# RWKV attention and routed experts in one kernel: a unit's scores masked in blocks of 64 tokens, the bonus term put on their diagonal

## The chip, the cores and the metric

The kernel runs as one program on one core of a Trainium2 chip. The metric is the device time of one execution in microseconds (us), taken as the median of several runs; lower is better. Engines are called PE (TensorE), DVE (VectorE), ACT (ScalarE), POOL (GpSimd) and SP (SyncE, which here only issues DMAs and reads registers). PSUM is the memory that PE writes into, in banks of 512 float32 columns on 128 partitions; SBUF holds everything else.

## What is computed

An RWKV attention over 4 batches, 8 heads of 48, 768 tokens, and then a mixture of 8 experts in which each of the 3072 tokens goes to one expert:

```python
for t in range(S):                                   # attention, per batch and head
    kt, vt, rt = k[:, :, t], v[:, :, t], r[:, :, t]
    cur = einsum('bhd,bhe->bhde', u * kt, vt)
    y[:, :, t] = einsum('bhd,bhde->bhe', rt, state + cur)
    state = w[..., None] * state + einsum('bhd,bhe->bhde', kt, vt)
x = y as (3072, 384)
logits = x @ w_gate + modality_bias[modality_id]     # experts
e_idx = argmax(logits); gate_w = softmax(logits)[e_idx]
for e in range(8):
    mask = e_idx == e
    out[mask] = gate_w[mask] * (relu(x[mask] @ w1[e]) @ w2[e])
```

## The kernel before, in words

The attention is computed in 24 units of 128 tokens (one of 4 batches, one of 6 chunks). Token t's own key enters with the factor u, all earlier ones of the chunk with powers of w; chunks before it come in through a state of 48 x 48 per head. A unit's value is so a sum of three parts: scores of the chunk with itself, masked to s < t, times v; the state times r; and the diagonal part, d v, where d is a number per token and head (the sum of r u k, "bonus").

For unit i the parts are, with the names that the code and the trace use:

- `keys_turned` and `keys` (L349, L399): k turned by PE into `pkT`, multiplied on DVE by powers of w into `kc`. `rc` (L361, POOL) is r with such powers.
- `scores` (L442): 16 matmuls of 64 keys by 128 tokens into two banks `psc` (heads of even number in one, of odd number in the other; the two partition halves of `kc` that hold them are two row halves of PE).
- `causal` (L448): two DVE products of 128x512 with the mask, out of PSUM into `at`.
- `values`: into the bank `py` first the state part (L472, eight matmuls, 96 columns), then `at` times v (L479, 16 matmuls of 128 keys, 64 tokens, 48 columns); then into the bank `pst` the state of the next chunk (L488 the old one faded, L493 keys times values; for units 4 to 13 both are on PE), and in the same bank the bonus of the next unit (L408).
- `taken` (L416): DVE copies the bonus out of `pst` as `d`. `own` (L428): ACT multiplies v by d, head by head, into `dv` (eight products of 128x48); for units 9 to 13 POOL does the second half (L424).
- `token` (L501, L516): DVE adds `dv` to `py`, then ACT squares the row and sums it. A power of two near its size (`factor`, L311 and L313 on DVE, `sx`) scales the row, which is kept as two float16 halves: `high` on ACT (L549), `low` on DVE (L553). `raised` (L562) turns it on PE, `flipped` (L577) copies it out on ACT.
- `settled_state` (L531, L539): ACT copies the new state from `pst` to `st`.

The order on each engine is written by hand in `run`: it is a loop over units, and in iteration i unit i's values stand beside unit i+1's scores and masks, unit i−1's row, unit i+2's keys, unit i+3's `rc`. All instructions of an engine run in the order in which they are written. Two or three "fills" in an iteration take the next instruction of a generator that computes routing (logits, the expert of a token, its place, its send to DRAM with an indirect DMA on POOL). In iterations 9 to 13 the weights of the first expert are split too, each sixth of them by ACT into `whi` (L1000) and by DVE into `wlo` (L1005); loads of these weights are issued by SP in iterations 3 to 10 (`halves`), after SP has waited for `d` and `sx` of the unit (`pace`). From 165 us on only experts' work is left.

In the setup and the first iterations run the small tables: `wd` (L217, four ACT products) and `tri` (L220), the faded state's factors and a triangle used in routing; their generator is drained by the same fills, behind `first`, which computes where the experts' rows begin.

Of the kernel before, what the change touches and what calls it, by code (L numbers as in the profile page):

```python
# [9 lines left out]
F32 = mybir.dt.float32  # L10
# [8 lines left out]
P = 128  # L19
# [6 lines left out]
E = 8  # L26
# [20 lines left out]
SHARED = range(9, 14)  # L47
TURNED = range(1, 15)
RAISED = range(4, 12)
OWNED = range(17, 24)  # L50

# [14 lines left out]
class _Kernel:  # L66
# [16 lines left out]
    def setup(self):  # L83
# [58 lines left out]
        nc.gpsimd.affine_select(self.mask, self.ones, pattern=[[1, P]], compare_op=ALU.is_gt, fill=0.0, base=0, channel_multiplier=-1)  # L142
        self.counts()
# [266 lines left out]
    def taken(self, i):  # L410
        u = self.ctx_[i]
        u["d"] = self.a.tile([P, H], F32, tag="d", name=f"d{i}", bufs=4)
        if i in OWNED:
            self.nc.vector.reduce_sum(u["d"], u["rk"].rearrange("p (h e) -> p h e", e=D), axis=AX.X)
            return
        self.nc.vector.tensor_copy(u["d"], u["pd"])  # L416

    def own(self, i, q):
        nc, u = self.nc, self.ctx_[i]
        if q == 0:  # L420
            u["dv"] = self.a.tile([P, DM], F32, tag="dv", name=f"dv{i}")
        if q and i in SHARED:
            half = lambda t: t[:, DM // 2 :].rearrange("p (h e) -> p h e", e=D)
            nc.gpsimd.tensor_mul(half(u["dv"]), half(u["v"]), u["d"][:, H // 2 :].unsqueeze(2).to_broadcast([P, H // 2, D]))  # L424
            return
        for h in range(q * H // 2, (q + 1) * H // 2):
            sl = slice(h * D, (h + 1) * D)
            nc.scalar.activation(u["dv"][:, sl], u["v"][:, sl], AF.Copy, scale=u["d"][:, h : h + 1])  # L428

    def scores(self, i):  # L430
# [7 lines left out]
        for pr in range(NPR):  # L438
            for q in range(2):
                s = slice(64 * q, 64 * q + 64)  # L440
                for j, r in enumerate(HALVES):
                    nc.tensor.matmul(u["ps"][j][s, pr * P : (pr + 1) * P], u["kc"][r, pr, s], u["rc"][r, pr, :], start=True, stop=True)  # L442

    def causal(self, i, j):
        nc, u = self.nc, self.ctx_[i]
        if j == 0:
            u["at"] = self.a.tile([P, H, P], F32, tag="at", name=f"at{i}")
# [14 lines left out]
    def values(self, i, beside=lambda: None):  # L462
# [3 lines left out]
        py = u["py"] = self.ps_y.tile([P, 512], F32, tag="y", name=f"py{i}")  # L466
        if c:
            for pr in range(NPR):
                c0 = pr * 2 * D
                for q in range(2):  # L470
                    t = slice(64 * q, 64 * q + 64)
                    nc.tensor.matmul(py[t, c0 : c0 + 2 * D], u["rc"][:112, pr, t], st[:112, b, pr, :], start=pr == 0, stop=False, skip_group_check=True)  # L472

        for h in range(H):
# [22 lines left out]
    def token(self, i):  # L497
# [3 lines left out]
        nc.vector.tensor_add(u["x"], u["x"], u["dv"])  # L501
# [87 lines left out]
    def choose(self, u):  # L589
# [7 lines left out]
        xinv = a.tile([P, B, 2], F32, tag="xinv", name=f"xinv{lo}")[:, :n, 0]  # L597
# [3 lines left out]
        nc.vector.reduce_sum(L, lg.rearrange("p g w e -> p g e w"), axis=AX.X)  # L601
        yield
        nc.vector.scalar_tensor_tensor(L, L, self.wginv, eb(xinv), ALU.mult, ALU.mult)
# [6 lines left out]
        bank = lambda c, w=E: u["pr"][:, c : c + n * w].rearrange("p (g w) -> p g w", g=n)  # L610
# [14 lines left out]
        zs = new("zs", 1)  # L625
# [19 lines left out]
    def place(self, u):  # L645
# [9 lines left out]
        pos = a.tile([P, B], F32, tag="pos", name=f"pos{lo}")[:, :n]  # L655
# [501 lines left out]
    def run(self):  # L1157
# [26 lines left out]
        def plan(step, f):  # L1184
            at.setdefault(step, []).append(f)
# [6 lines left out]
        halves = {3: (0, 1), 4: (2,), 5: (3, 4), 6: (5,), 7: (6,), 8: (7, 8), 9: (9, 10), 10: (11,)}  # L1192

        def half(i, at):
            for q in halves.get(i, ())[at : at + 1]:
                if q == 0:
                    self.eid = nc.sync.value_load(self.ctl[:, :1], min_val=0, max_val=E - 1)
                self.load(self.eid, 2 * NQ, q)
# [8 lines left out]

        routing = self.setup2()
        plan(0, lambda: next(routing))
        plan(1, lambda: next(routing))  # L1210
        plan(1, lambda: fills.append(chain(self.first(), routing, self.first_order())))
# [355 lines left out]
```

## Time and profile before

| | us |
|---|---|
| three runs | 340.17, 343.05, 343.06 |
| median | 343.05 |
| the profiled execution's own time | 344.49 |
| its span | 342.8 |
| PE busy | 325.1 (95% of the span) |
| DVE busy | 216.1 (63%) |
| ACT busy | 180.6 (53%) |
| POOL busy | 161.8 (47%) |

The span runs from the first to the last instruction that the profile holds; some 1.7 us of the execution lie outside it. The units take about the first 165 us, the experts the rest. Busy PE means that a matmul is in flight, at either of the two clock levels; the granted clock says how far it ran below 2.4 GHz.

### The profile page before, as it was taken

To read this page: it belongs to the slowest core of one execution; us is meant where nothing else is said; L and a number is where in the kernel's file an instruction comes from. 1 tells how busy PE (TensorE), PEld (TensorE's weight loads), DVE (VectorE), ACT (ScalarE), POOL (GpSimd) and SP (SyncE) were. 2 spreads that over 40 slices of the span, in tenths; PEclk is the share of its full clock that TensorE was granted. 3 is DMA by queue.
4 is the path that set the end of the run, shared out by engine and by line. 5 is a ranking of instruction groups with operands and counts; after the bars stand their busy time and mean duration, and the time that the engine had idled before them with its cause. 6 is when DMAs were issued, how large, how long until landed. Compare 5 with 4: busy or idle time off the path is not lost. (4 is left out here: it accounts for less than half of the span.)

```text
span 342.8 us, 15268 instructions
## 1 busy us (share of the span) xinstructions
PE 325.1 (95%) x5471; PEld 264.7 (77%) x5471; DVE 216.1 (63%) x748; ACT 180.6 (53%) x483; POOL 161.8 (47%) x237
## 2 busy tenths in 40 slices
PE   8997999889999999999998999998999999999992
PEld 3787888788888888797886788876888877777671
DVE  8966986989997987787666523377333332333950
ACT  7759799685874758577421222264222225542820
POOL 8967787986949786344458211202211111111211
PEclk9999999989999999999999999999999999999998
DMA  6767967655799999973366541118512211122110
GB/s 187 233 144 207 248 228 225 207 156 132 169 219 205 270 283 235 217 175 96 86 110 240 148 72 46 46 46 288 154 46 63 52 46 23 46 68 47 36 46 5
DMA packets 56414, 47.55 MB, mean 139 GB/s; under 512 B 40744, under 2 KB 49207, under 8 KB 56112
## 3 DMA queue, kind: packets, MB, share of 16 engines
q1 hardware_dynamic: 53168, 37.45, 45.7%
q0 software_dynamic: 3200, 9.47, 7.6%
q8 instruction: 31, 0.51, 0.6%
q14 instruction: 15, 0.12, 0.1%
HBM read 27.21 MB, written 11.83 MB: 114 GB/s over the span
## 5 line engine op out<-in xcount | busy, mean ns | idle before, releaser
L1059 PEld LDWEIGHTS <-whi 128*128 128x128 f16 x1248 | 72.4, 98 | 4.3 <-issue 1.0
L1068 DVE SCALAR_TENSOR_TENSOR hl<-phb,hh 128x256 f16<-128x256 f32 (+1 forms) x48 | 24.5, 511 | 69.6 <-issue 36.4
L1122 PEld LDWEIGHTS <-hh 128*128 128x128 f16 x416 | 39.0, 98 | 28.6 <-ACT hh L1063 2.0
L1059 PE MATMUL phb<-mxT,whi 128*128 128x128 f16 x768 | 51.0, 219 | 0.2
L428 ACT ACTIVATE dv<-kv,d 128x48 f32<-128x48 f32 x172 | 43.1, 325 | 1.1 <-DVE d L416 1.0
L1063 ACT ACTIVATE hh<-phb 128x256 f16<-128x256 f32 (+1 forms) x48 | 21.4, 454 | 41.0 <-PE phb L1059 18.6
L1059 PEld LDWEIGHTS <-wlo 128*128 128x128 f16 x624 | 37.8, 98 | 0.0
L1028 POOL TENSOR_TENSOR seenb<-otb,putb 128x1 int32<-128x1 int32 x16 | 4.4, 273 | 66.7 <-ACTq L1498 53.2
L448 DVE TENSOR_TENSOR at<-psc,mask 128x512 f32<-128x512 f32 x48 | 31.8, 681 | 0.2 <-PE psc L442 0.2
L685 POOL DMA_INDIRECT rows<-row,posi x24 | 26.5, 1105 | 11.0 <-DVE base L661 3.1
L1122 PEld LDWEIGHTS <-hl 128*128 128x128 f16 x208 | 19.4, 98 | 15.3 <-issue 2.5
L361 POOL TENSOR_TENSOR rc<-ud,powr 112x512 f32<-112x512 f32 (+1 forms) x25 | 30.6, 1226 | 0.8 <-PE py L472 0.4
L1122 PE MATMUL po<-whi,hh 128*128 128x384 f16 x136 | 27.7, 326 | 2.0 <-ACT whi L1000 1.2
L1059 PE MATMUL phb<-mxT,wlo 128*128 128x128 f16 x384 | 29.3, 219 | 0.0
L1122 PE MATMUL po<-whi,hl 128*128 128x384 f16 x136 | 28.0, 326 | 1.2 <-PEq L1563 0.7
L442 PE MATMUL psc<-rc,kc 48*64 48x128 f32 (+1 forms) x768 | 27.8, 280 | 0.2
L1122 PE MATMUL po<-wlo,hh 128*128 128x384 f16 x136 | 27.7, 326 | 0.0
L1059 PE MATMUL phs<-mxT,whi 128*128 128x128 f16 x432 | 27.2, 219 | 0.0
L1019 ACT ACTIVATE otb<-po,fac 128x384 f32<-128x384 f32 x16 | 9.3, 579 | 33.8 <-PE phb L1059 33.8
L479 PE MATMUL py<-kv,at 128*64 128x48 f32 x768 | 26.9, 223 | 0.0
L1005 DVE SCALAR_TENSOR_TENSOR wlo<-raw,ws,whi 128x1024 f16<-128x1024 f32 (+1 forms) x20 | 25.9, 1313 | 1.3 <-issue 0.6
L442 PEld LDWEIGHTS psc<-rc,kc 48*64 48x64 f32 (+1 forms) x768 | 21.3, 134 | 6.2 <-issue 2.8
(288 smaller groups left out, 639.2 us busy)
## 6 DMA issues: line engine op xcount, KB each, us to landing
kv<-in_pt SPq DMA_DIRECT2D x21, 384.0 KB
ud<-in_pd SPq DMA_DIRECT2D x10, 384.0 KB
raw<-in_w SPq DMA_DIRECT2D x12, 256.0 KB
raw<-in_w SPq DMA_DIRECT2D x6, 512.0 KB
raw<-in_w SPq DMA_DIRECT2D x2, 1536.0 KB, 6.4
ud<-in_pd SPq DMA_DIRECT2D x14, 192.0 KB
rows<-pad SPq DMA_DIRECT2D x10, 193.0 KB
rt<-in_pt SPq DMA_DIRECT2D x7, 192.0 KB
```

Source lines behind the costliest of these rows:

```text
L361: nc.gpsimd.tensor_mul(u["rc"][:TOP, s], u["rT"][:TOP, s], self.powr[:TOP, s])
L428: nc.scalar.activation(u["dv"][:, sl], u["v"][:, sl], AF.Copy, scale=u["d"][:, h : h + 1])
L442: nc.tensor.matmul(u["ps"][j][s, pr * P : (pr + 1) * P], u["kc"][r, pr, s], u["rc"][r, pr, :], start=True, stop=True)
L448: nc.vector.tensor_mul(u["at"][:, j * NPR : (j + 1) * NPR, :], u["ps"][j].rearrange("p (q t) -> p q t", q=NPR), self.mask.unsqueeze(1).to_ ...
L479: nc.tensor.matmul(py[t, sl], u["at"][:, j * NPR + pr, t], u["v"][:, sl], start=c == h == 0, stop=h == H - 1, skip_group_check=True)
L685: i = nc.gpsimd.indirect_dma_start(out=self.rows, out_offset=bass.IndirectOffsetOnAxis(ap=u["posi"][:, b : b + 1], axis=0), in_=u["row"][: ...
L1005: self.nc.vector.scalar_tensor_tensor(self.wlo[:, sl], self.raw[:, sl], sc, self.whi[:, sl], ALU.mult, ALU.subtract)
L1019: self.nc.scalar.activation(ot, po[:, :DM], AF.Copy, scale=gf[:, t : t + 1])
L1059: self.nc.tensor.matmul(ph[:, q * P : (q + 1) * P], w[:, c0 : c0 + P], self.xT[:, xq, t * P : (t + 1) * P], start=i == q == 0, stop=i == l ...
L1063: self.nc.scalar.activation(self.hh[:, f0 : f0 + fb, t * P : (t + 1) * P], p3, AF.Relu)
L1068: self.nc.vector.scalar_tensor_tensor(self.hl[:, f0 : f0 + fb, r], p3, 0.0, self.hh[:, f0 : f0 + fb, r], ALU.max, ALU.subtract)
L1122: self.nc.tensor.matmul(po[:, :DM], h[:, f, t * P : (t + 1) * P], w[:, c0 : c0 + DM], start=first, stop=last)
```

## The change

`BANDED` is the set of units 9 to 13; for them

- the masked scores are no longer one 128 x 128 block per head. They are kept as `band`, the two 64 x 64 blocks on the diagonal (the keys of the same 64 tokens, one above the other on the partitions), and `past`, the block of the later 64 tokens with the earlier 64 keys, which needs no mask. The block above the diagonal isn't computed.
- `scores` writes 64 instead of 128 columns for the second half of the keys, and its result is laid out by block, head and token.
- `causal` multiplies on DVE only `band` (128x256 for each bank) with a 64-column mask; ACT copies `past` (64x256 for each bank). The lower half of `past` is zeroed by POOL, for units 9 and 10 only: `at` becomes two fixed tiles used in turn.
- `taken` puts the bonus on the diagonal of `band` by a predicated copy on DVE (mask `eye`, 128x512) out of the bank `pst`, instead of copying 128x8.
- `own` does nothing (no `dv`), and `token` has no add.
- `values` begins with 16 matmuls of `band` (64 keys, 64 tokens, 48 columns), then the state part, then eight of `past` (128 partitions, 64 tokens, 48 columns).

For all units: `eye` and the 64-column mask are four ACT copies in the setup; small results of routing (`xinv`, `zs`, `pos`) lie in PSUM columns and the sum of the logits in SBUF; the generator with `wd` and `tri` is interleaved with steps 2 to 6 of `first`; and the loads of the first expert's weight halves begin one slot later.

```diff
-SHARED = range(9, 14)
+BANDED = range(9, 14)
@@ setup
+        self.att = [c.tile([P, H, P], F32, name=f"at{q}") for q in range(2)]
+        self.band, self.eye = (c.tile([P, P // 2], F32, name=n) for n in ("band", "eye"))
+        for q in range(2):
+            t = slice(64 * q, 64 * q + 64)
+            nc.scalar.copy(self.eye[t], id32[t, t])
+            nc.scalar.copy(self.band[t], self.mask[t, t])
@@ taken
+        if i in BANDED:
+            to = [P, 2, NPR, P // 2]
+            self.nc.vector.copy_predicated(
+                u["band"].rearrange("p (j a) t -> p j a t", j=2),
+                self.eye.bitcast(I32).unsqueeze(1).unsqueeze(1).to_broadcast(to),
+                u["pd"].rearrange("p (a j) -> p j a", j=2).unsqueeze(3).to_broadcast(to),
+            )
+            return
@@ own
+        if i in BANDED:
+            return
-        if q and i in SHARED:
-            half = lambda t: t[:, DM // 2 :].rearrange("p (h e) -> p h e", e=D)
-            nc.gpsimd.tensor_mul(half(u["dv"]), half(u["v"]), u["d"][:, H // 2 :].unsqueeze(2).to_broadcast([P, H // 2, D]))
-            return
@@ scores
+                    if i in BANDED:
+                        to = u["ps"][j][s].rearrange("p (w a t) -> p w a t", w=2, a=NPR)[:, : 2 - q, pr]
+                        nc.tensor.matmul(to, u["kc"][r, pr, s], u["rc"][r, pr, 64 * q :].rearrange("p (w t) -> p w t", w=2 - q), start=True, stop=True)
+                        continue
@@ causal
-            u["at"] = self.a.tile([P, H, P], F32, tag="at", name=f"at{i}")
+            u["at"] = self.att[i % 2]
+        if i in BANDED:
+            if j == 0 and i - 2 not in BANDED:
+                nc.gpsimd.memset(u["past"][64:], 0.0)
+            s, half = slice(j * NPR, (j + 1) * NPR), u["ps"][j].rearrange("p (w a t) -> p w a t", w=2, a=NPR)
+            nc.vector.tensor_mul(u["band"][:, s], half[:, 0], self.band.unsqueeze(1).to_broadcast([P, NPR, P // 2]))
+            nc.scalar.copy(u["past"][:64, s], half[:64, 1])
+            return
@@ values
+        for h in range(H if i in BANDED else 0):
+            pr, j = divmod(h, 2)
+            sl = slice(h * D, (h + 1) * D)
+            for t in (slice(0, 64), slice(64, P)):
+                nc.tensor.matmul(py[t, sl], u["band"][t, j * NPR + pr, :], u["v"][t, sl], start=h == 0, stop=False, skip_group_check=True)
...
+            nc.tensor.matmul(py[64:, sl], u["past"][:, j * NPR + pr, :], u["v"][:, sl], start=False, stop=h == H - 1, skip_group_check=True)
@@ token
-        nc.vector.tensor_add(u["x"], u["x"], u["dv"])
+        if i not in BANDED:
+            nc.vector.tensor_add(u["x"], u["x"], u["dv"])
@@ choose
-        xinv = a.tile([P, B, 2], F32, tag="xinv", name=f"xinv{lo}")[:, :n, 0]
+        xinv = col(448)
-        nc.vector.reduce_sum(L, lg.rearrange("p g w e -> p g e w"), axis=AX.X)
+        raw = new("lgs")
+        nc.vector.reduce_sum(raw, lg.rearrange("p g w e -> p g e w"), axis=AX.X)
@@ run
-        halves = {3: (0, 1), 4: (2,), 5: (3, 4), 6: (5,), 7: (6,), 8: (7, 8), 9: (9, 10), 10: (11,)}
+        halves = {3: (None, 0), 4: (1, 2), 5: (3, 4), 6: (5,), 7: (6,), 8: (7, 8), 9: (9, 10), 10: (11,)}
-        plan(1, lambda: fills.append(chain(self.first(), routing, self.first_order())))
+        plan(1, lambda: fills.append(chain(beside(self.first(), routing, 2, 5), routing, self.first_order())))
```

On DVE, in iteration 10, the rows around the split of a sixth of the first expert's weights (`wlo`). Before:

```order
L1005 SCALAR_TENSOR_TENSOR wlo<-raw,ws,whi 128x1024
L501 TENSOR_TENSOR py_1509<-py_1509,dv_1492 128x384
L827 TENSOR_SCALAR skip<-again_1507 128x1
L416 COPY d_1622<-pst_1534 128x8
L598 TENSOR_SCALAR xinv_1632<-sx_877 128x4
```

After, as far as the masked products of the next unit:

```order
L1041 SCALAR_TENSOR_TENSOR wlo<-raw,ws,whi 128x1024
L863 TENSOR_SCALAR skip<-again_1501 128x1
L424 COPY_PREDICATED at_157<-eye,pst_1536 128x512
L634 TENSOR_SCALAR pr_1561<-sx_887 128x4
L855 TENSOR_SCALAR done<-done,fur_0_1482 128x1
L405 TENSOR_TENSOR kc_1639<-pkT_1596,powk 112x512
L317 TENSOR_SCALAR ebx_1641<-ssq_1444 128x1
L638 TENSOR_REDUCE lgs_1643<-pr_1561 128x32
L319 TENSOR_SCALAR sx_1445<-ebx_1641 128x1
L857 TENSOR_SCALAR off<-done 128x1
L469 TENSOR_TENSOR at_158<-psc_0_1601,band 128x256
L640 SCALAR_TENSOR_TENSOR pr_1561<-lgs_1643,wginv,pr_1561 128x32
```

The add behind `wlo` is gone, the predicated copy stands where the small copy of `d` stood, and the masked product has 256 columns instead of 512.

On PE, the values of unit 10, between the scores of unit 11 (`psc`) and the faded state (`pst` from `wd`). Before:

```order
L442 MATMUL psc_0_1599<-rc_1326,kc_1474 64x128
L442 MATMUL psc_1_1600<-rc_1326,kc_1474 64x128
L472 MATMUL py_1668<-st_98,rc_1189 64x96 x8
L479 MATMUL py_1668<-kv_89,at_1498 64x48 x16
L488 MATMUL pst_1693<-st_98,wd 64x48
```

After:

```order
L456 MATMUL psc_0_1601<-rc_1323,kc_1472 64x64
L456 MATMUL psc_1_1602<-rc_1323,kc_1472 64x64
L495 MATMUL py_1663<-kv_89,at_157 64x48 x16
L501 MATMUL py_1663<-st_98,rc_1188 64x96 x8
L506 MATMUL py_1663<-kv_89,at_157 64x48 x8
L521 MATMUL pst_1696<-st_98,wd 64x48
```

The 16 matmuls with `at` stand ahead of the state part instead of behind it (they are those of `band`), and eight more, those of `past`, stand behind it.

On ACT, the end of iteration 2 and the beginning of iteration 3. Before:

```order
L531 COPY st_99<-pst_461 48x4x48
L428 ACTIVATE dv_543<-kv_91,d_518 128x48 x4
L549 ACTIVATE row_402<-py_444,sx_405 128x384
L428 ACTIVATE dv_543<-kv_91,d_518 128x48 x4
L516 ACTIVATE row_402,ssq_404<-py_562 128x384
L531 COPY st_99<-pst_579 64x4x48
L217 ACTIVATE wd<-id_150,w_186 112x112
L531 COPY st_99<-pst_579 48x4x48
L217 ACTIVATE wd<-id_150,w_186 112x112 x3
```

After:

```order
L565 COPY st_99<-pst_466 48x4x48
L223 ACTIVATE wd<-id_150,w_194 112x112 x3
L440 ACTIVATE dv_552<-kv_91,d_523 128x48 x4
L583 ACTIVATE row_408<-py_449,sx_411 128x384
L223 ACTIVATE wd<-id_150,w_194 112x112
L226 CAST tri<-mask 128x128
L440 ACTIVATE dv_552<-kv_91,d_523 128x48 x4
L550 ACTIVATE row_408,ssq_410<-py_573 128x384
L565 COPY st_99<-pst_590 64x4x48
```

All of `wd` and `tri` stand one iteration earlier: in front of and between the products of `dv`, no longer between the state copies.

## Rows read from the trace of the kernel before

**Rows 1.** The page's busy times of each engine, with share and instructions.
```profile
PE 325.1 (95%) x5471; PEld 264.7 (77%) x5471; DVE 216.1 (63%) x748; ACT 180.6 (53%) x483; POOL 161.8 (47%) x237
```

**Rows 2.** Windows by stage; columns as in its second line.
```profile
core 0: us, PE busy (x) PEld busy (x) DVE busy (x) ACT busy (x) POOL busy (x), PEclk, DMA share, GB/s
...
59.00:75.00 16.00, 13.61 (x343) 12.37 (x340) 15.08 (x47) 11.99 (x32) 14.39 (x14) 0.89 0.59 184
75.00:98.00 23.00, 22.54 (x550) 20.09 (x546) 22.36 (x66) 15.92 (x39) 16.62 (x15) 1.00 0.74 166
98.00:165.00 67.00, 66.96 (x1306) 56.14 (x1306) 53.01 (x185) 44.16 (x142) 41.26 (x51) 1.00 0.90 209
```

**Rows 3.** Windows: five units, and two pieces of unit 10 and 11's iterations.
```profile
56.85:91.54 34.69, 31.85 (x810) 29.38 (x809) 31.70 (x99) 26.24 (x66) 28.94 (x27) 0.95 0.61 174
66.13:70.39 4.26, 2.61 (x59) 2.18 (x59) 4.26 (x16) 4.23 (x9) 3.82 (x5) 1.00 0.92 272
70.39:74.64 4.25, 4.25 (x81) 3.92 (x82) 3.33 (x14) 3.12 (x11) 3.94 (x5) 0.60 0.33 99
```

**Rows 4.** Timeline of PE, 56 to 83: unit 9's values, then waits of iteration 10.
```profile
57.99 0.88 PE L472 MATMUL py<-st,rc 112*64 112x96 f32 x16
58.70 1.09 PE L479 MATMUL py<-kv,at 128*64 128x48 f32 x32
59.62 0.57 PE L488 MATMUL pst<-st,wd 112*64 112x48 f32 x15
...
66.13 0.61 PE L488 MATMUL pst<-st,wd 112*64 112x48 f32 x15 [0.74 <-ACT st L539]
...
69.68 0.34 PE L562 MATMUL pxT<-id,row 128*128 128x128 f16 x3 [1.01 <-DVE row L553]
```

**Rows 5.** Waits, 56 to 98: us in total, times, longest.
```profile
ACT row L516 <- DVE py L501: 9.8, 5, 3.5
```

**Rows 6.** Timeline of DVE, 59 to 75.
```profile
60.46 0.67 DVE L448 TENSOR_TENSOR at<-psc,mask 128x512 f32<-128x512 f32 x1
...
62.07 2.40 DVE L1005 SCALAR_TENSOR_TENSOR wlo<-raw,ws,whi 128x1024 f16<-128x1024 f32 x1
64.39 0.55 DVE L501 TENSOR_TENSOR py<-py,dv 128x384 f32<-128x384 f32 x1
...
64.92 0.15 DVE L416 COPY d<-pst 128x8 f32<-128x8 f32 x1
64.99 1.43 DVE L598 TENSOR_SCALAR xinv<-sx 128x4 int32<-128x4 int32 x1
...
69.71 1.26 DVE L1005 SCALAR_TENSOR_TENSOR wlo<-raw,ws,whi 128x1024 f16<-128x1024 f32 x1
```

**Rows 7.** Timelines: DVE late in the kernel, and POOL from 59 to 70.
```profile
168.30 0.16 DVE L598 TENSOR_SCALAR xinv<-sx 128x3 int32<-128x3 int32 x1
...
200.63 0.42 DVE L1068 SCALAR_TENSOR_TENSOR hl<-pha,hh 128x256 f16<-128x256 f32 x1
...
62.09 1.28 POOL L361 TENSOR_TENSOR rc<-ud,powr 112x512 f32<-112x512 f32 x1
...
65.38 1.00 POOL L368 TENSOR_TENSOR kt<-kv,wtok 128x384 f32<-128x384 f32 x1
```

**Rows 8.** Timeline of ACT, 56 to 72: iteration 10.
```profile
65.46 0.62 ACT L539 COPY st<-pst 64x192 f32<-64x192 f32 x2
66.10 0.80 ACT L577 COPY xT<-pxT 128x768 f16<-128x768 f16 x1
...
67.71 0.56 ACT L549 ACTIVATE row<-py,sx 128x384 f16<-128x384 f32 x1
68.18 1.14 ACT L1000 ACTIVATE whi<-raw,ws 128x1024 f16<-128x1024 f32 x1
```

**Rows 9.** Timeline of PE, 17.9 to 20.8: single matmuls with 128 columns of weights.
```profile
17.96 0.38 PE L213 MATMUL pswg<-wgssq,ones 128*128 128x1 f32 x2
18.20 0.63 PE L349 MATMUL pkT<-id,kv 128*112 128x128 f32 x4
```

**Rows 10.** Timeline of PE, 26 to 46: start, busy, line, idle before.
```profile
29.97 0.88 PE L472 MATMUL py<-st,rc 112*64 112x96 f32 x16 [0.41 <-DVE wgs L313]
...
32.35 0.61 PE L488 MATMUL pst<-st,wd 112*64 112x48 f32 x15 [0.58 <-ACT st L531]
...
37.55 0.61 PE L488 MATMUL pst<-st,wd 112*64 112x48 f32 x15 [0.20 <-ACT st L539]
...
45.50 0.34 PE L562 MATMUL pxT<-id,row 128*128 128x128 f16 x3 [0.26 <-DVE row L553]
```

## What the change is predicted to do

> **What bounds the kernel now.** I read the page's busy times first, then the windows by stage, then the PE timeline, the waits, and the other engines where PE stood. PE is busy 95% of the span, the next engine, DVE, 63% [rows 1]. So a unit is worth what PE does in it, plus what PE waits. The stages differ: from 75 to 98 us PE leaves 0.46 of 23 us open, from 98 to 165 us 0.04 of 67, but from 59 to 75 us 2.39 of 16, and there DVE is busy 15.08 of 16 and the granted clock averages 0.89 [rows 2]. Since PE has next to no slack from 83 us on, what is won or lost before carries to the end.
>
> PE multiplies with `at` of units 9 to 13 in the stretch 56.85 to 91.54 us: 34.69 us, PE busy 31.85, so 2.84 idle. In 70.39 to 74.64 the granted clock was 0.60, that is, for much of it the lower level of 1.2 GHz, right after a stretch in which PE was busy for 2.61 of 4.26 us [rows 3]. The work in that slow piece (scores, state, at·v) took 4.25 us; in iteration 9 it took 59.62 − 56.85 = 2.77 [rows 3, 4], of which some 0.1 was a matmul of the expert weights' scale: 1.59 lost. There are four waits of over 0.3 us in this stretch (those at 66.13 and 69.68 stand in the rows), and each also hides some 0.2 us in which the last matmul's drain counts as busy. Sum: 2.84 + 1.59 + 4 × 0.2 = **5.2 us** that PE loses there; its bare work is 29.5 us, or 5.9 a unit.
>
> What is late there? PE at 66.13 waits for ACT's state copy, at 69.68 for DVE's half of `row` [rows 4], and between them for ACT's half. ACT's own large wait is the Square behind DVE's add of `dv`: five times, 9.8 us, the longest 3.5 [rows 5]. And that add is late because `wlo` is ahead of it on DVE: 2.40 us beside POOL's `rc` at 62.09, with the add at 64.39 [rows 6, 7]. So the chain is wlo, add, Square, state copy, PE.
>
> **Removed.** In each of five units: DVE's add, 0.55 [rows 6]; four ACT products for one half of `dv` and POOL's one product for the other. None is PE work, so alone they are worth only PE's waits behind them. With the add gone Square and the state copies behind it no longer stand behind `wlo` through the add. But the predicated copy now stands in the same place on DVE, behind `wlo`, and reads the bank that the state copy reads. I take it that ACT waits for it, where today it waits for the 0.15 copy of `d` only after the add [rows 6].
>
> **Added on DVE.** The two masked products shrink from 128x512 to 128x256: 0.67 [rows 6] against 0.42, the nearest 256-column row [rows 7]; 2 × 0.25 = 0.5 off. The copy of `d`, 0.15, becomes a predicated copy of 128x512. No row has one: bounds 0.42 (as 256 columns) and 1.35 (twice a 512-column row); I take 0.70, nearest to the 512-column product that also reads PSUM and a broadcast. DVE per unit: −0.55 − 0.5 + (0.70 − 0.15) = −0.5. Since DVE has no slack at 59 to 75 us, that is 0.5 more air where PE waits.
>
> **Added on ACT.** Two past copies of 64x256, about 0.35 each by the 64x192 state copies, 0.31 [rows 8], against four products less: no heavier. In the iteration before unit 9 ACT gets only the copies, +0.7, hidden by Square's waits, of which the mean is 9.8 / 5 = 2 us [rows 5]. Two memsets on POOL follow `kt` of the next unit, three units ahead of the need; unhidden they would cost the first past matmul of units 9 and 10 at most a `kt` each, 1.0 [rows 7]. Four copies in the setup sit beside DVE's decay tables; uncovered, 0.3 each by the same state copies.
>
> **PE.** Old at·v: 16 matmuls, 32 records, two column halves side by side, 58.70 to 59.62 = 0.92. The 16 band matmuls are 16 pairs of records again, now of two row halves with a column half each: I take 0.92 again, ends 0.71 (state's pace) and 1.84 (not side by side). Then eight past matmuls come on top, 16 single records, on one column half with nothing beside. Lower end: state's 16 records take 57.99 to 58.70, 0.71 [rows 4]. Upper end: two single matmuls with 128 columns of weights start 0.24 apart for both, 17.96 to 18.20, 0.12 each, half for 64 columns, 0.06 × 16 = 0.96 [rows 9]. Chosen **0.85**, near the 0.92 of at·v. Scores lose half their columns in half of the matmuls; I give that nothing (at best −0.2), since their pace is that of weights and starts. PE: 5 × 0.85 = **+4.25**, with past's ends 3.55 to 4.8.
>
> A page of the Trainium skill ("TensorEngine Tiling (Array Packing)", Restrictions and Gotchas, Gotcha 1) says that two row tiles can't reach one PSUM bank at once and that they are to write to different banks. The kernel before has its row halves (the scores) in two banks, so no row here shows it; by that rule the band matmuls would run one after the other, and the sum would be that of the first rival below.
>
> **Is PE still held up?** The loop that remains runs through DVE and ACT: predicated copy 0.7, state copies 0.62, turned copy of `row` 0.8, scaled `row` 0.56, past copies 0.7, `whi` 1.14 [rows 8], then `wlo`, 1.26 or, beside POOL, 2.40 [rows 6], and the next predicated copy: 5.8, or 6.9 beside POOL. PE has 5.9 + 0.85 = 6.75 on average. So PE leads in most units and I leave 0.5 of the 5.2 us as remaining waits. What the new wait can hold up: behind band on PE stand state, past, fade and all later matmuls. Between the bonus, which the predicated copy reads, and band PE does at least the next scores, 56.85 to 57.99, 1.1 us, against a copy of 0.7: that holds unless `wlo` is still running when the bonus ends.
>
> **The small steps.** From 29 to 46 us PE idles behind DVE or ACT for 0.41 (a `py` bank), 0.58, 0.20 and 0.26 us [rows 10], each with about 0.2 more as drain: 0.6 + 0.8 + 0.4 + 0.45 = 2.25. `xinv` took 1.43 us at 64.99, beside POOL's `kt` from 65.38, and 0.16 at 168.30 with three columns and POOL done with such work [rows 6, 7]: with its result in PSUM I take 0.2. The `wd` products move one iteration up on ACT, ahead of `dv`, so Square of unit 2 and the state copies behind it come later there. I take 1.5 of the 2.25 us as gone, since the wait at 32.35 keeps half and the later Square takes up to 0.3; ends 0.6 and 2.1. The first expert's weight halves load one slot later on SP; 98 to 165 us has no PE idle that they could lengthen [rows 2], and unless a norm meets a half still in flight they cost nothing; if one does, ACT's norm moves, by at most a slot.
>
> **Sum**, against the profiled run of 344.49 (its span 342.8, the rest outside): −1.5 − (5.2 − 0.5) + 4.25 = **−2.0**, 342.5. That run is 0.4% above the median of 343.05, so on the median's scale −2.0 gives **341.0**. With all terms at their good ends (2.1, 5.2, 3.55) it is −3.75, with all at their bad ones (0.6, 3.2, 4.8) +1.0: the likeliest case's own range is 339.3 to 344.1.
>
> **Rivals.** (a) Slower: the two row halves of a band do not run side by side in one bank. Price +0.92 a unit, ×5 = 4.6; then −2.0 + 4.6 = +2.6, 345.7, and past at its upper end another 1. Break-even is at 6.2 / 5 = 1.25 us of PE more per unit; against 0.85 that takes only 0.4 on top. For: both halves write one bank, as the scores don't. Against: their partitions are disjoint. Chance 0.15. (b) Faster by more: past 0.71, band 0.71, scores −0.2, nearly all 5.2 gone: −1.8 − 5.2 + 5 × (0.71 − 0.21 − 0.2) = −5.5, 337.6. For: band loads 64 rows of weights, not 128; against: by the rows pace goes with the count of matmuls. Chance 0.25. (c) No gain: the predicated copy at 1.2 to 1.35 behind a long `wlo` makes band wait 0.3 to 0.6 in each unit and the state copy with it: 2 to 3 of the 5.2 stay, +0.5, 343.5. For: DVE was 15.08 of 16 busy. Against: 0.5 us of masking less. Chance 0.2. The forecast itself (d) has 0.4.
>
> A median of this kernel can tell about 1% from no change (its runs spread 340.17 to 343.06). 1% is 339.6 and 346.5. Faster: nearly all of (b) and an eighth of (d) = 0.3; slower: two thirds of (a), where past is at its upper end or a wait stays = 0.1; the rest the same, 0.6. Range for eight in ten, which leaves out half of (a) and the far side of (b): 337.3 to 345.5.
>
> **What would show it.** Band: the run of 16 matmuls into `py` 0.9 us (1.8: rival a). Past: 0.85 for eight. The predicated copy near 0.7. ACT's Square no longer released by DVE in units 9 to 13; PE's waits at the state copies and `row` of unit 9 and 10 gone and the clock at 1.00 throughout 59 to 92 us; the 34.69 us of five units at 34.2. `xinv` 0.2. After 98 us PE as before. The forecast falls if PE's five units take over 36 us, or if a later stage, 98 to 165, takes other than 67.

## The result, and the profile after

The change made the kernel slower: 344.25 us (median of 18 runs, 342.06 to 346.71) against 342.09 (18 runs, 339.88 to 348.01). The ratio is 1.0081, 95% interval 1.0056 to 1.0106: about 2.8 us more by the ratio (2.2 by the medians), where 2.0 less was forecast. The time lies inside the stated range and within the 1% that was called "no change"; its sign is the other one.

The two profiled executions can't be subtracted as they stand: that of the kernel before took 344.49 us, over its median, that of the changed one 342.06, the lowest of its runs. The reading is therefore by stage, between the first scores matmul of one unit and of another on PE (read from PE's timelines; the last row goes to the end of PE's last matmul, behind which some 5.7 us of the span lie), for two executions of each kernel:

| stage (start of scores of unit) | before | before again (e8) | after | after again (e7) |
|---|---|---|---|---|
| to unit 6 | 34.42 | 34.43 | 34.47 | 33.74 |
| 6 to 10 | 22.43 | 23.57 | 22.62 | 22.67 |
| 10 to 15, values of units 9 to 13 | 34.69 | 34.55 | 35.50 | 35.53 |
| 15 to 23 | 61.30 | 61.26 | 60.64 | 61.25 |
| 23 to the end | 184.25 | 181.06 | 181.33 | 181.74 |

The last row is what made the first profile of before long: 184 or 181 us, without any change (e13 and e14 below, on a chip where the kernel before took 345.31, have 184 too). The page's busy times hardly moved, PE's up and DVE's down (compare [rows 1]):

```profile
PE 325.6 (96%) x5551; PEld 266.7 (78%) x5551; DVE 211.0 (62%) x743; ACT 180.4 (53%) x477; POOL 159.4 (47%) x234
```

The other rows of the table matter. Up to unit 10 the first pair of executions gains nothing (57.09 for 56.85), where 1.5 us less was forecast for the small steps; the second pair does (56.41 for 58.00), but e8 has a stretch at the lower clock there, shown below. The five units are 0.8 to 1.0 longer where 0.45 less was forecast.

First the five units, as a window of the changed kernel (columns as in [rows 2]), against 34.69 in [rows 3]; then ACT's and PE's waits there:

```profile
57.09:92.59 35.50, 34.30 (x891) 32.01 (x890) 31.45 (x99) 25.75 (x56) 27.94 (x24) 1.00 0.62 178
```
```profile
ACT st L573 <- DVE at L424: 6.2, 3, 2.9
...
PEld py L495 <- DVE at L424: 1.1, 2, 0.8
```

The clock is at 1.00 there (0.95 in [rows 3]) and PE idles 1.20 us instead of 2.84, yet the stage is longer: PE is busy for 34.30 us instead of 31.85. Square's wait of [rows 5] is gone; in its place ACT's state copies wait for DVE's predicated copy, and twice PE does, at band (0.15 and 0.51 us; 0.80 and 0.54 in e7; another 0.50 of the 1.20 is a stop that the profile puts down to nothing, "issue"). PE's timeline shows unit 9's values and both waits, and a last row, of the kernel before, where its bonus begins:

```profile
58.23 1.14 PE L495 MATMUL py<-kv,at 64*64 64x48 f32 x32
59.29 0.88 PE L501 MATMUL py<-st,rc 112*64 112x96 f32 x16
60.01 0.91 PE L506 MATMUL py<-kv,at 128*64 128x48 f32 x13
...
61.65 0.61 PE L414 MATMUL pst<-uw,rk 112*64 112x2 f32 x16
...
65.57 1.13 PE L495 MATMUL py<-kv,at 64*64 64x48 f32 x32 [0.15 <-DVE at L424]
...
72.02 1.14 PE L495 MATMUL py<-kv,at 64*64 64x48 f32 x32 [0.51 <-DVE at L424]
```
```profile
60.45 0.21 PE L408 MATMUL pst<-uw,rk 112*64 112x2 f32 x1
```

Band takes 58.23 to 59.29, 1.06 us, against 0.92 for the old at·v ([rows 4]). Past, the faded state and the new state together take 60.01 to 61.65, 1.64, against 0.83 without past (59.62 to the bonus at 60.45 in the trace of before): past is 0.81, that is, so much longer is the stretch. So PE does 0.14 + 0.81 = 0.95 us more in each unit, 4.75 in five.

On DVE's timeline of iteration 10 (compare [rows 6]) the order is wlo, predicated copy, `xinv`, and then the masks of unit 11; the last two rows are wlo and the copy of iteration 11:

```profile
62.17 2.64 DVE L1041 SCALAR_TENSOR_TENSOR wlo<-raw,ws,whi 128x1024 f16<-128x1024 f32 x1 [0.47 <-ACT whi L1036]
...
64.80 0.72 DVE L424 COPY_PREDICATED at<-eye,pst 128x512 f32<-128x512 int32 x1
65.41 0.17 DVE L634 TENSOR_SCALAR pr<-sx 128x4 int32<-128x4 int32 x1
...
66.50 0.41 DVE L469 TENSOR_TENSOR at<-psc,band 128x256 f32<-128x256 f32 x1
...
69.08 2.15 DVE L1041 SCALAR_TENSOR_TENSOR wlo<-raw,ws,whi 128x1024 f16<-128x1024 f32 x1 [0.70 <-ACT whi L1036]
...
71.25 0.70 DVE L424 COPY_PREDICATED at<-eye,pst 128x512 f32<-128x512 int32 x1
```

Now the early stage. PE reaches the first logits at 38.59, 0.45 us sooner than before (39.04, the last row below), and then stops for the rows of the fourth unit, which a transposing DMA brings into `xT`:

```profile
38.59 0.61 PE L621 MATMUL pr<-wghl,xT 128*128 128x16 f16 x18
40.81 0.31 PE L621 MATMUL pr<-wghl,xT 128*128 128x16 f16 x6 [1.61 <-DMA xT<-row]
```
```profile
39.04 1.02 PE L587 MATMUL pr<-wghl,xT 128*128 128x16 f16 x24
```

SP's queue suggests why. Two weight halves (`raw`, 256 KB each) and a `kv` now stand right ahead of this transposing DMA (the fourth of the kernel; the expectations below count from 20 us and call it the third), where the kernel before had one half and a `kv`. It is issued at 35.10 and lands 5.7 us later; the last three rows are the queue of the kernel before:

```profile
33.51 0.34 SPq L1002 DMA_DIRECT2D raw<-in_w  x1
34.05 0.39 SPq L346 DMA_DIRECT2D kv<-in_pt  x1
34.64 0.35 SPq L1002 DMA_DIRECT2D raw<-in_w  x1
35.10 1.83 SPq L603 DMA_TRANSPOSE xT<-row  x1
```
```profile
xT<-row SPq DMA_TRANSPOSE x1, 5.7
```
```profile
32.55 0.34 SPq L966 DMA_DIRECT2D raw<-in_w  x1
33.21 0.39 SPq L340 DMA_DIRECT2D kv<-in_pt  x1
35.52 1.24 SPq L569 DMA_TRANSPOSE xT<-row  x1
```

### The profile page after: what moved, and what is told of

Read it like the earlier page. It is cut to its first block, busy times and chain, and to the rows that moved or that the text cites. A ratio compares the mean times of both kernels' runs of the same rounds, so it can differ in the third digit from the quotient of the medians.

```text
span 340.3 us, 15410 instructions
## 1 busy us (share of the span) xinstructions
PE 325.6 (96%) x5551; PEld 266.7 (78%) x5551; DVE 211.0 (62%) x743; ACT 180.4 (53%) x477; POOL 159.4 (47%) x234
## 5 line engine op out<-in xcount | busy, mean ns | idle before, releaser
L440 ACT ACTIVATE dv<-kv,d 128x48 f32<-128x48 f32 x152 | 38.0, 325 | 1.3 <-DVE d L430 1.0
L1041 DVE SCALAR_TENSOR_TENSOR wlo<-raw,ws,whi 128x1024 f16<-128x1024 f32 (+1 forms) x20 | 26.8, 1361 | 3.8 <-ACT whi L1036 3.0
L472 DVE TENSOR_TENSOR at<-psc,mask 128x512 f32<-128x512 f32 x38 | 25.1, 680 | 0.3 <-PE psc L458 0.2
L392 POOL TENSOR_TENSOR rk<-rc,kc 112x512 f32<-112x512 f32 x13 | 16.6, 1275 | 17.0 <-DVE ebx L317 9.1
L1005 ACT ACTIVATE junk<-raw 128x1024 f16<-128x1024 f32 x18 | 18.9, 1051 | 7.5 <-PE po L1158 7.4
L458 PE MATMUL psc<-rc,kc 64*64 64x128 f32 x608 | 21.3, 276 | 0.6 <-POOL rc L367 0.4
```

The costliest lines, as they stand in the source:

```text
L392: nc.gpsimd.tensor_mul(u["rk"][:TOP], u["rc"][:TOP], u["kc"][:TOP])
L472: nc.vector.tensor_mul(u["at"][:, j * NPR : (j + 1) * NPR, :], u["ps"][j].rearrange("p (q t) -> p q t", q=NPR), self.mask.unsqueeze(1).to_ ...
L1005: self.nc.scalar.activation(junk, self.raw[:, q * WQ : (q + 1) * WQ], AF.Square, accum_out=self.ssq[:, q : q + 1])
L1041: self.nc.vector.scalar_tensor_tensor(self.wlo[:, sl], self.raw[:, sl], sc, self.whi[:, sl], ALU.mult, ALU.subtract)
```

## The experiments

All ratios are to the kernel before, run beside it on the same chip. The stages are those of the one execution of each whose trace is at hand, read as above (us); the median is that of all its runs, so the two don't always agree. Ratios are compared across chips too: e1 to e4 ran on one, e5 to e8 on a second, e9 to e12 on a third, e13 and e14 on a fourth, where the kernel before takes 345.31. e7 and e8 stand in the table above.

| | median, ratio (95%) | to 6 | 6 to 10 | 10 to 15 | 15 to 23 | to the end |
|---|---|---|---|---|---|---|
| e1 small steps only | 345.18, 1.0100 (1.0053 to 1.0148) | 33.98 | 26.07 | 35.68 | 60.65 | 180.98 |
| e2 band only | 344.29, 1.0118 (1.0063 to 1.0173) | 34.78 | 22.05 | 36.52 | 61.40 | 181.87 |
| e3 after, old loads | 344.99, 1.0097 (1.0068 to 1.0126) | 33.79 | 21.65 | 35.52 | 61.42 | 181.66 |
| e4 before, wlo later | 340.12, 0.9971 (0.9944 to 0.9999) | 34.44 | 22.33 | 34.15 | 60.65 | 181.04 |
| e5 e4 and steps, old loads | 341.67, 1.0013 (0.9987 to 1.0039) | 34.05 | 24.43 | 33.57 | 60.64 | 180.97 |
| e6 after, past twice | 349.33, 1.0233 (1.0189 to 1.0277) | 34.21 | 22.93 | 38.85 | 60.64 | 182.13 |
| e9 after, no load in 4 | 342.73, 1.0050 (1.0016 to 1.0084) | 34.55 | 22.02 | 35.50 | 61.43 | 181.46 |
| e10 e4, steps, no load in 4 | 339.94, 0.9956 (0.9920 to 0.9993) | 34.16 | 21.93 | 33.97 | 60.64 | 181.13 |
| e11 after, wlo later | 344.57, 1.0094 (1.0063 to 1.0125) | 34.30 | 25.05 | 33.62 | 60.65 | 181.47 |
| e12 diagonal in 128x128 scores | 344.92, 1.0087 (1.0056 to 1.0117) | 33.83 | 25.41 | 36.75 | 60.64 | 180.80 |
| e13 after, wlo later, no load in 4 | 345.82, 1.0003 (0.9977 to 1.0029) | 34.16 | 23.06 | 34.18 | 61.54 | 184.84 |
| e14 before, no load in 4 | 345.08, 1.0007 (0.9980 to 1.0035) | 34.38 | 22.42 | 34.71 | 61.42 | 184.37 |

**Halves of the change.** e1 is the kernel before with the last five pieces of the diff alone (routing, `beside`, `halves`); e2 is it with the rest alone. The first question was on which side the loss is.

> The kernel before with the small steps alone: xinv, zs and pos in PSUM, wd and tri moved, weight halves one slot later; units 9 to 13 as before. Theory A: the move of the loads puts two 256 KB weight halves directly ahead of the transposing DMA into xT, PE waits 1.0 to 1.7 us for it at the first logits, and that eats the waits that the steps remove, so 0 to +0.8 us against before. Theory B: the steps gain what was forecast, 1.5 us, and all that was lost lies in units 9 to 13: -1.0 to -2.0 us.

> The kernel before with the banded units alone, loads and routing as before. Theory A: PE's work grows by 0.95 us a unit, 4.75 in five, and 2.5 to 3 us of waits go: +1.7 to +2.5 us against before. Theory B: all of the loss is here and the small steps gained 1.5: +3.5 to +4.5 us.

They came out at +1.0% and +1.2%, 3.4 and 4.0 us. e1 lies over both of its theories. e2 lies over its first and has the number of its second, but that one had the small steps gain. Each half is slower by itself, and together they are more than the whole change. e1's trace shows what the estimate had left out. PE waits for `xT` longer still, and right behind the wait its clock is at the lower level (PE's timeline, then a window):

```profile
41.33 0.32 PE L587 MATMUL pr<-wghl,xT 128*128 128x16 f16 x6 [2.05 <-DMA xT<-row]
```
```profile
39.80:46.60 6.80, 5.27 (x70) 4.60 (x72) 3.23 (x14) 3.53 (x12) 3.07 (x5) 0.51 0.84 251
```

PE's 5.27 busy us of that window, at a granted clock near 0.5, cost some 2.6 us on top of the wait of 2. e2 has no such wait, and its loss lies in units 9 to 13: 36.52 us at full clock, longer than in the whole change, where PE waits 2.0 us at band in two places; its `xinv` is still in SBUF and takes 1.37 us on DVE in iteration 10, and the masked products of unit 11 come 1.1 us later than in the changed kernel (67.56 for 66.50). 15 to 23 and the end add about 0.9 against e8.

**The loads.** e3 puts the old table back into the changed kernel; e9 leaves iteration 4 without any load.

```diff
-        halves = {3: (None, 0), 4: (1, 2), 5: (3, 4), 6: (5,), 7: (6,), 8: (7, 8), 9: (9, 10), 10: (11,)}
+        halves = {3: (0, 1), 4: (2,), 5: (3, 4), 6: (5,), 7: (6,), 8: (7, 8), 9: (9, 10), 10: (11,)}   # e3
+        halves = {3: (0, 1), 5: (2, 3), 6: (4, 5), 7: (6,), 8: (7, 8), 9: (9, 10), 10: (11,)}          # e9
```

> The changed kernel with only the table of the weight halves put back, so that one load, not two, stands right ahead of the third transposing DMA on SP. Theory A: PE's wait of 1.6 us for xT at the first logits goes, and the time falls by 1.0 to 1.6 us against the changed kernel: +1.0 to +1.8 us against before. Theory B (the wait is an accident of that one run, or the gap is given back by a later wait): as the changed kernel within 0.5 us, +2.3 to +3.2 against before.

> The changed kernel with no weight half loaded in iteration 4, so that no 256 KB load stands on SP between the second and the third transposing DMA; those halves come in iterations 5 and 6. In the traces so far the third transposed block lands 4.6 us after its issue with one such load ahead (e8) and 5.7 to 5.8 with two. Theory A (the queue in front of it): it lands in under 4 us, PE's wait at the first logits goes from 1.8 to under 0.3 us, a fall of the clock behind it goes too: -1.5 to -3 us against the changed kernel, -0.2 to +1.3 against before. Theory B (the transposing itself takes that long, whatever is ahead): the wait stays over 1 us and the time as the changed kernel's, +2.2 to +3.2.

e3 is not conclusive. In its trace the wait for `xT` fell from 1.61 to 0.64 us and the stage 6 to 10 to 21.65, but that execution took 341.79 us and was the lowest of ten; the median did not fall (1.0097). So the shift of the table by one slot is not shown to cost time by itself. In e9 the wait is gone in the trace, and the median is 342.73, 0.5% over before instead of 0.8%, which is 1.1 us by the ratios and 1.5 by the medians; that is over theory A's range, under theory B's, and the intervals of the two ratios overlap, so e9 alone does not settle it. Two other pairs below differ in the loads of these iterations, and each moves clear of noise: e5 to e10 (1.0013 to 0.9956) and e11 to e13 (1.0094 to 1.0003). SP's queue ahead of the same DMA and PE's first logits in e9:

```profile
33.43 0.38 SPq L346 DMA_DIRECT2D kv<-in_pt  x1
35.11 1.22 SPq L603 DMA_TRANSPOSE xT<-row  x1
```
```profile
38.67 0.97 PE L621 MATMUL pr<-wghl,xT 128*128 128x16 f16 x24
```

PE starts the logits at the same time as in the changed kernel (38.67 for 38.59), the DMA is issued at the same time (35.11 for 35.10), and only the loads ahead of it are missing: 24 matmuls in one row, no wait. The mean granted clock over all runs went from 0.990 (changed kernel, 18 runs) to 0.995 (12 runs); 0.005 of 342 us is up to 1.7 us of PE's time, where PE sets the end. Wait and clock together could so be worth up to 3.3 us; measured are 1.1 to 1.5, so if both went in full, part of them is given back elsewhere.

Over all sixteen traces the wait goes with the loads of iteration 4: 0 to 0.41 us in the four without one, 0.11 to 1.34 in the six with one, 1.49 to 2.05 in the six with two. Among the kernels that have the small steps the order is the same: 0 to 0.41 (e9, e10, e13), 0.64 and 1.34 (e3, e5), 1.49 to 2.05. And the clock goes with the wait. Six kernels wait 1.3 us or more in their trace (the changed one, e1, e5, e6, e11, e12); over all their runs the granted clock averages 0.985 to 0.990. The other eight, the kernel before among them, average 0.991 to 0.995. That is a comparison of kernels and not a test, but it fits the traces in which the clock falls behind the wait.

**A second trace of each kernel.**

> The changed kernel once more, for a second trace. If the wait at the first logits for the transposed rows is part of it, it stands there again, 1.0 to 2.2 us; PE's five units take 35 to 36 us where the clock is full; if the run is near the median of 344.25, a stretch at the lower clock level or a wait that the first trace lacked accounts for 2 us.

> The kernel before once more, for a second trace: near its median of 341 to 342 us, with no wait at the first logits, the waits at the state copy and at row of iteration 10 again, and the time behind unit 23 near 181 us, as in the other traces, not 184.

e7 (342.69 us) has the wait again, 1.65 us, and 35.53 in the five units. It does not have the stretch at the lower clock that the median would need; e1, e5, e11 and e12, which share the steps, have it behind the same wait, e6, with a wait of 1.51, does not. e8 (342.27 us) was expected without a wait there and has one: the kernel before is on its edge. With one weight half ahead the block lands 4.6 us after its issue, PE waits half a microsecond, and the clock falls then too, as well as in iteration 11, where the first profile had it. Its DMA issue, PE's row and two windows:

```profile
xT<-row SPq DMA_TRANSPOSE x1, 4.6
```
```profile
40.14 0.31 PE L587 MATMUL pr<-wghl,xT 128*128 128x16 f16 x6 [0.49 <-DMA xT<-row]
```
```profile
71.57:75.60 4.03, 4.03 (x81) 3.70 (x82) 3.11 (x14) 3.08 (x11) 3.73 (x5) 0.63 0.36 103
40.14:43.50 3.36, 3.36 (x48) 2.92 (x48) 3.06 (x10) 3.01 (x8) 2.41 (x6) 0.54 0.83 280
```

The kernel before has the fall in iteration 11 in both of its traces, the changed one in neither. But over all runs the two average nearly the same granted clock, 0.990 (the 18 runs of the changed kernel) and 0.991 (the 96 runs of the one before beside the experiments), so what the change wins there it must lose elsewhere, and its 2.8 us are not a difference of the clock.

**The price of past.** e6 adds eight more matmuls of its shape, with weights of zero, ahead of those of past.

```diff
+        for h in range(H if i in BANDED else 0):
+            sl = slice(h * D, (h + 1) * D)
+            nc.tensor.matmul(py[64:, sl], self.zero, u["v"][:, sl], start=False, stop=False, skip_group_check=True)
```

> The changed kernel with eight more matmuls of past's shape in each of units 9 to 13, with weights of zero. If PE is the bound of these units and nothing gives time back later, the price of past itself, 0.81 us a unit by the trace, is seen in full: +3.5 to +4.2 us against the changed kernel, +6.5 against before. If DVE and ACT were the bound there, half of it or less would be seen: under +2 us.

+1.5% against the changed kernel (1.0233 / 1.0081), 5.2 us, more than the 3.5 to 4.2 of the first theory. The five units in its trace take 38.85 us, 3.35 more than 35.50, and PE hardly idles in this window:

```profile
57.14:95.99 38.85, 38.54 (x970) 36.82 (x970) 32.44 (x98) 25.54 (x55) 29.79 (x25) 1.00 0.60 164
```

That is about the 4.05 of 5 × 0.81 less what the added work covers of the waits (PE idles 0.31 us there instead of 1.20). What PE's work adds there is not given back later. The other 1.8 us of the median are not explained; the end is 0.4 to 0.8 longer in this trace.

**The waits.** e4 moves one thing in the kernel before, e11 the same in the changed one: DVE's wlo is issued behind `taken` of the next iteration.

```diff
-        split = lambda q: lambda: self.split(q)
+        split = lambda q: lambda: (self.wide(q), owed.append(q)) if q < 4 else self.split(q)
+        owed = []
...
             each(i, self.taken) if i else None
+            while owed:
+                self.fine(owed.pop(0))
```

> The kernel before; only wlo of units 9 to 12 is issued on DVE behind the add of dv and the copy of d of the next iteration instead of ahead of them. If what PE lost in units 9 to 13 was Square and the state copies waiting behind wlo through that add, the waits at the state copy and at row go without any more work for PE: -1.5 to -3 us against before. If DVE's total is the bound there, the waits move to row's second half or to the next masks, and the time stays within 0.7 us.

> The changed kernel with wlo of units 9 to 12 behind the predicated copy on DVE. PE's waits for the predicated copy at band (0.4 to 0.8 twice, 1.9 us with their drain in both traces) then go: -1.2 to -2 us against the changed kernel, +0.8 to +1.6 against before, and PE's five units take 33.6 to 34.3 us. If the waits come from DVE's total work, they move and the time stays within 0.5 us of the changed kernel's.

e4 is 0.3% faster, 1.0 us, between the two forecasts. Its trace has no wait for the state copy or for `row` in iteration 10 any more, but stops of PE of 0.5 and 1.2 us in the middle of bursts, put down to "issue" and so to nothing that the profile shows, and a lower clock behind them; the five units still took 34.15. e11 did what was expected in the units and not in the total; its windows of the five units and of the stretch behind the first logits:

```profile
59.35:92.97 33.62, 33.62 (x890) 31.97 (x889) 30.83 (x98) 25.38 (x56) 27.48 (x24) 1.00 0.69 188
41.50:45.00 3.50, 3.49 (x50) 2.82 (x50) 1.77 (x9) 2.79 (x8) 1.41 (x4) 0.56 1.04 351
```

33.62 us, with PE busy in all of it: 1.9 less than the changed kernel. But the wait for `xT` is there, with the clock at 0.56 behind it, and 6 to 10 takes 25.05. So both were removed at once (e13), and, to know what the loads do by themselves, the table of e9 was put alone into the kernel before (e14):

> The changed kernel with wlo later and no weight half in iteration 4. Theory A (two separate causes that add): 1.5 us (e9) plus 1.9 us (PE's five units in e11) under the changed kernel: -0.9 to +0.5 us against before. Theory B (PE's extra 0.95 us a unit sets the end whatever is done about waits, and e11's gain is given back later): as e9, +1.2 to +2.3 against before.

> The kernel before with the same table of loads as e9 and e10 alone. Theory A: PE of the kernel before reaches the first logits half a microsecond later than the changed one and waits there for 0 to 0.5 us, so the table is worth little: -0.7 to 0 us. Theory B (the table helps by itself, by other transfers): -1.2 to -2 us.

e13 stands at 1.0003, e14 at 1.0007. With both waits out, the changed kernel is level with the one before. The two do not simply add: against the changed kernel's 1.0081, e9 alone took off 0.3%, e11 alone nothing, and both together 0.8%. What does nothing while the wait for `xT` stands (e11) is worth 0.5% once that is gone (e9 to e13, 1.0050 to 1.0003, just clear of noise). And the table of loads does nothing for a kernel whose PE comes later to the logits.

**The diagonal without the past matmuls.** e12 keeps the 128x128 scores, masks and matmuls of before and sets the diagonal with two predicated copies:

```diff
-            to = [P, 2, NPR, P // 2]
+            to = [64, 2, NPR, P // 2]
+            for q in range(2):
+                t = slice(64 * q, 64 * q + 64)
+                self.nc.vector.copy_predicated(
+                    u["at"][t, :, t].rearrange("p (j a) t -> p j a t", j=2),
+                    self.eye[t].bitcast(I32).unsqueeze(1).unsqueeze(1).to_broadcast(to),
+                    u["pd"][t].rearrange("p (a j) -> p j a", j=2).unsqueeze(3).to_broadcast(to),
+                )
```

> The changed kernel with the 128x128 masked scores kept in units 9 to 13 (scores, masks and 16 matmuls as before) and the diagonal put into them by two predicated copies of 64x512: no add, no dv, and no past. PE's extra work of 0.95 us a unit goes, DVE gets 1.2 us a unit more. If PE's extra matmuls are what made the change slower: -2 to -4 us against the changed kernel, about +0.5 to -1 against before. If DVE is the bound there, its 1.2 us more shows in the units: as the changed kernel or up to 2 us slower.

The second theory: 1.0087. The window of the five units has DVE busy 35.47 of 36.75 us, and PE waits in the middle of at·v, at `row` and at the routing; below it the two copies on DVE's timeline:

```profile
59.24:95.99 36.75, 32.51 (x811) 29.51 (x810) 35.47 (x102) 22.09 (x44) 26.53 (x22) 0.95 0.58 169
```
```profile
67.06 1.47 DVE L426 COPY_PREDICATED at<-eye,pst 64x512 f32<-64x512 int32 x2
```

In the units the changed kernel so traded one bound for another: with the blocks PE is busy for 34.30 of 35.50 us, with the diagonal alone DVE for 35.47 of 36.75. The ratio by itself doesn't say so, since e12 keeps the shifted loads, with a wait of 1.49 us for `xT` and a stage 6 to 10 of 25.41.

**A version that beats both.** e5 and e10 are the kernel before with wlo later and the small steps, e5 with the old loads, e10 with none in iteration 4.

> The kernel before with wlo later (as e4) and the small steps, but with the old table of weight halves. e4 alone was 0.3% faster. Theory A (the small steps gain about 1 us by unit 8, and it was the moved loads that lost it): -1.5 to -2.5 us against before. Theory B (in e1 the small steps themselves lost, since PE then reaches the first logits before their transposed rows have landed, waits there, and its clock falls after the wait): 0 to +3 us.

> The kernel before with wlo later and the small steps, and no weight half in iteration 4. Theory A: what e5 lost in a wait of 1.3 us for the transposed rows and the clock behind it comes back: -1.5 to -3 us against e5, so -0.8 to -2.2 against before, the best so far. Theory B: as e5, -0.4 to +1.3.

e5: as theory B, no gain; PE waits 1.34 us for `xT`, at the lower clock afterwards. Only one half stands ahead of the DMA there, and yet the block lands 6.0 us after its issue:

```profile
40.62 0.31 PE L587 MATMUL pr<-wghl,xT 128*128 128x16 f16 x6 [1.34 <-DMA xT<-row]
```
```profile
xT<-row SPq DMA_TRANSPOSE x1, 6.0
```

The DMA is issued 0.9 us sooner there than in e8 and lands half a microsecond later, so the number of loads ahead is not all that decides.

e10 takes 339.94 us, 0.4% faster than before (0.9920 to 0.9993) and 1.2% faster than the changed kernel by the ratios (0.9956 / 1.0081). Its gain sits in 6 to 10, 21.93 us instead of 22.43 or 23.57, and in the five units. It has no banded scores. e13 is the same with them (and with the rest of the change), and stands 0.5% higher (1.0003 for 0.9956, just clear of noise, on another chip): where both have the same small steps, wlo and loads, the blocks cost time.

## Why the prediction was wrong

- **Past and band, +4.25.** Right in kind and near in size: past 0.81 for 0.85, band 1.06 for 0.92, so +4.75. e6 shows that it is paid in full.
- **Predicated copy 0.70, masks 0.42, `xinv` 0.2.** Measured 0.72, 0.41 and 0.17.
- **"5.2 us that PE loses there", of which 0.5 were to stay.** The units now take 35.50, that is 29.5 + 4.75 + 1.25: 3.95 went, not 4.7. The failing step is "that holds unless `wlo` is still running when the bonus ends": it is, in units 10 and 11, where the copy stands behind a wlo of 2.64 and 2.15 us. The copy took over the add's place in the queue together with its wait, which was named, and in the sum had no price but the 0.5 kept for all waits. e11 takes that wait away and gets 33.62. With work and wait the units are 0.8 to 1.0 us longer, not 0.45 shorter; e2, the units alone, is 1.2% slower.
- **The small steps, −1.5.** This is the other failing step: alone (e1) they are 1.0% slower. The waits at 29.97, 37.55 and 45.50 of [rows 10] did go. The sum then lets that gain run on to the end, and says of the weight halves that "unless a norm meets a half still in flight they cost nothing". I had looked for who uses the loads, not for what is queued behind them on SP: a transposing DMA whose block PE needs some 4 us after its issue. Even without the shift the block was due when PE came (e8, e5), so a gain ahead of that point could not come through whole. The wait is 1.6 us, more than the 0.45 that PE was ahead, and in several traces the clock falls behind it (e1, e5, e11, e12). With no load in iteration 4 it goes: 0.3% in the changed kernel (e9, not clear of noise), 0.6% from e5 to e10, 0.9% from e11 to e13. That the shift by one slot is what costs, rather than any load there, is not shown: e3, with the old table, is no faster.
- **"After 98 us PE as before."** Held within 0.7 us for 15 to 23. The end is longer in all traces with banded units, 181.33 to 182.13 against 180.80 to 181.13 without (184.84 against 184.37 on the chip of e13 and e14; the first profile's 184.25 stands apart); where that is from stays open.
- **The signs of being wrong.** The prediction would have fallen with over 36 us in the units or with other than 67 from 98 to 165. The units took 35.50: neither sign looked at the stretch ahead of the units.
- **The rivals.** (a) gave +2.6, near what was measured, by a mechanism that did not happen; that is luck. (c), the copy behind wlo, is in the trace, with a copy of 0.72 instead of 1.2 to 1.35. No rival had a DMA in it.
- **What the sum was made against.** An execution with 184 us behind unit 23 and one stretch of low clock; neither was a reason for the miss, since only differences were taken from it, but the waits of one execution were taken as those of all.

What stays open: why the two halves of the change (e1, e2) lose more together than the whole, why e3's median did not follow its trace, the last 1.8 us of e6, why the same block lands so differently, and how often the clock falls behind the wait in the changed kernel itself, whose two traces do not have it.

## What to carry to other kernels

When a load is moved, read the queue that issues it and ask what stands behind it there; its own user is the smaller question. A gain ahead of a point where the bounding engine meets a DMA is worth no more than the DMA's lead, and behind a wait at that point a stretch of lower clock can follow, as in e1 and e8. An operation that takes another's place in a queue takes over its wait; here moving the long instruction behind it took the wait away (e4, e11).

## What the runs showed of the hardware

- A matmul that fills one column half costs nearly as much as a pair that fills both: 32 records of band in pairs take 1.06 us, of at·v 0.92, and 16 single ones of past 0.81. Cutting the masked quarter of a block saved PE nothing: the scores of unit 10 take 1.03 us with it (56.85 to 57.88) and without (57.09 to 58.12).
- The row halves of band write one PSUM bank, on disjoint partitions, and run side by side: 1.06 us for 16 pairs, where one after the other was put at 1.84. The Trainium skill ("TensorEngine Tiling (Array Packing)", Restrictions and Gotchas) says that different row tiles can't access one bank at the same time; for disjoint partitions the trace does not bear that out.
- A predicated copy of 64x512 takes as long as one of 128x512: 1.47 us for two against 0.72 for one.
- The same small transposing DMA landed 4.6 us after its issue in e8 and 6.0 in e5, each with one load of 256 KB ahead of it in its queue, and 5.7 in the changed kernel with two.
